# Attention and a gated two-layer product: wide differences from GpSimd to VectorE, wider fillers, one score step moved

## The chip, the cores and the metric

The kernel runs on one core of one Trainium2 chip. Its engines are TensorE (PE in the profile; PEld is its loading of weights), VectorE (DVE), ScalarE (ACT), GpSimd (POOL) and SyncE (SP), whose queue issues nearly all DMA transfers. The metric is the device time of one execution in microseconds (us); lower is better. The time before is 831.21 us, the median of three runs (831.0 to 831.5).

## The reference

Block-local softmax attention on 8 batches, 8 heads, 576 positions in chunks of 64, then a gated product on its result, all in float32:

```
scores = scale * matmul(q_c, k_c^T)                # per chunk of 64
attn   = exp(scores - max) ; attn = attn / (sum + 1e-9)
x      = matmul(attn, v_c)                         # 4608 tokens x 512
h      = x @ w_in                                  # 512 x 2048
g      = h * clip(h + 3, 0, 6) / 6
out    = g @ w_out                                 # 2048 x 512
```

## The kernel before

Precision comes from splitting: each operand is kept as a high part (a cast to fp32r on ACT) and a low part (operand minus high part, on DVE), and `passes` (L295 to L299) runs three matmuls per pair, high by high (L297), high by low (L298), low by high (L299). One such 128x512 matmul starts 0.227 us after the one before when PE runs freely; six of them make one part of a product, 1.36 us.

The 4608 tokens are nine blocks of 512. Each block has two attention units, named by block and half ("61" is the second half of block 6). A unit is a chain of steps: scores on PE (L222), maximum, difference (L229, L233) on DVE, exponential on ACT, sum with reciprocal, share (L240 to L245) on DVE, a transpose on PE (L255, "turn"), a copy on ACT (L259), the product with the values on PE (L273), and a copy to keep it (L280 or L283 on ACT, for the first three blocks also a residue, L286 on DVE).

Blocks 0 to 2 then go through the two matrix products tile by tile: sixteen tiles of weights (L166 loads them, `convert` makes high and low parts on ACT and DVE, the low part at L193), a first product a/b, a gate, a second product c. Blocks 3 to 8 are taken two at a time, in three stages s = 0, 1, 2, with seven products in place of eight for a 2x2 scheme of quarters. That costs additions and differences: of the operands x (`x_steps`, L432: four differences of 1024 columns in each stage), of the gated values (L687 and L689, 512 columns, on POOL; L711 on DVE and L714 on POOL, 1024 columns, four each in each stage), and of the results. Each operand of the second product is split by `add_units`: high on ACT (L704), low on DVE (L708). So a stage is a first product (56 parts, f), a change to the second product, and the second product (56 parts, s). While a stage changes over, one attention unit for the next stage is under way: unit 61 in stage 0, unit 81 in stage 1, none in stage 2.

In stage 0 the differences L432 run on DVE, in stages 1 and 2 on POOL; L714 runs on POOL in all three.

The order on each engine is made at build time. Every step is entered in a table with its engine, an assumed cost, what it waits for, and a due time; `Schedule.order` goes through them as a list scheduler does, and the instructions are then issued in that order. An assumed cost thus changes no instruction, but it can change the order. The engines run their own lists in order; they wait for each other only through data and buffers. SP's list is fixed the same way; the load of the next unit's q and k waits until the scores of the unit before have been computed, because there is one buffer.

Ahead of the first weight tile PE also runs fillers ("products on nothing", `warm_up`, L154): 11 at the very start, on zeros, 512 columns wide, and then a number in each of PE's planned pauses, `int(FILL * pause)`, with 256 columns of the identity.

Of the kernel before, what the change touches and what calls it, by code (L numbers as in the profile page):

```python
# [9 lines left out]
F32 = mybir.dt.float32  # L10
F32R = mybir.dt.float32r
BF16 = mybir.dt.bfloat16
# [3 lines left out]
ALU = mybir.AluOpType  # L16
AX = mybir.AxisListType

P = 128
# [4 lines left out]
NT = NB * CH  # L24
# [9 lines left out]
SLOTS = 7 * NFP  # L34
HALF = [slice(0, CH), slice(CH, P)]
WARM = 11
FILL = 6.5
LAG = 2
EDGE = 32
HASTE = 5.0  # L40
# [72 lines left out]
def tile_kernel(ctx: ExitStack, tc: tile.TileContext, qk_in, v_in, weights, out):  # L113
    nc = tc.nc
    PE, ACT, DVE, POOL = nc.tensor, nc.scalar, nc.vector, nc.gpsimd
# [8 lines left out]
    ps_h = pool("ps_h", 2, space=bass.MemoryType.PSUM)  # L124
# [10 lines left out]
    op = None  # L135

    nought = rp.tile([P, NT], F32, name="r")
    POOL.memset(nought, 0.0)
    ident = const.tile([P, P], F32, name="ident")
# [4 lines left out]
    ACT.activation(out=warm, in_=half, func=AF.Exp)  # L144


    some = ident.bitcast(BF16)

    def warm_up(n, a=some, b=some):
        if not n:  # L150
            return
        idle = ps_h.tile([P, NT], F32, name="h")[:, :b.shape[-1]]
        for _ in range(n):
            PE.matmul(idle, lhsT=a[:, :P], rhs=b, start=True, stop=True)  # L154

    nought = nought.bitcast(BF16)
    warm_up(WARM, nought, nought[:, P:P + 512])

# [262 lines left out]
    def operand():  # L423
        return xop_pool.tile([P, 2, 2, NT], F32R, name="xop")

    WHERE = {1: (0, 0), 5: (0, 1), 6: (0, 1), 7: (0, 0), 2: (1, 0), 3: (1, 1), 4: (0, 1)}

    def x_steps(s, eng):
        n = NSTD + 2 * s
        b = lambda i, j: xraw[n + j][:, i]  # L430
        name = lambda i: f"x{s}.{i}"
        minus = lambda to, x, y: lambda: eng.tensor_tensor(out=b(*to), in0=b(*x), in1=b(*y), op=ALU.subtract)  # L432
        sub = ("DVE", 1.3) if eng is DVE else ("POOL", 2.9)
        ops[s] = {}
        last = name("s0")
        steps = [(last, *sub, [], minus((0, 1), (0, 1), (0, 0)), [0, 1])]

        def high(i):
            ops[s][i] = operand()
            ACT.copy(out=ops[s][i][:, :, 0], in_=b(*WHERE[i]))  # L440

        def lower(i):
            DVE.tensor_tensor(out=ops[s][i][:, :, 1], in0=b(*WHERE[i]), in1=ops[s][i][:, :, 0].bitcast(F32), op=ALU.subtract)

        for i in ORDER_A:
            reads = {2: [3], 3: [2]}.get(i, [])
            steps.append((name(f"{i}h"), "ACT", 1.05, [last], lambda i=i: high(i), reads))
            steps.append((name(f"{i}l"), "DVE", 1.35, [name(f"{i}h")], lambda i=i: lower(i), []))
            for k, at, to, x, y, reads in (("s1", 5, (0, 1), (1, 1), (0, 1), [2]), ("s2", 6, (0, 0), (0, 1), (0, 0), []),
                                           ("s3", 6, (0, 1), (1, 0), (0, 1), [3])):  # L450
                if i == at:
                    steps.append((name(k), *sub, [name(f"{i}l"), name("1l"), last], minus(to, x, y), reads))
                    last = name(k)
        return steps
# [4 lines left out]
    work = Schedule()  # L459
# [7 lines left out]
    def attention(u, due, scores=(), less=(), keep=()):  # L467
        n, dp = int(u[0]), int(u[1])
        a = heads[u]
        steps = [("scores", "PE", 1.30, a.scores, ["qk" + u, *scores]), ("max", "DVE", 1.23, a.largest, ()),  # L470
                 ("less", "DVE", 1.23, lambda: a.lessen(spare.get("e" + u, lambda: None)()), less), ("exp", "ACT", 1.06, a.exp, ()),
                 ("sum", "DVE", 1.68, a.total, ()), ("share", "DVE", 1.22, a.share, ()), ("turn", "PE", 1.07, a.turn, ()),
                 ("turned", "ACT", 1.02, a.turned, ()), ("product", "PE", 1.50, a.product, ["v" + u]), ("keep", "ACT", 1.03, a.keep, keep)]
        if n < NSTD:
            steps.append(("rest", "DVE", 1.23, a.rest, ()))
        before = None
        for name, engine, cost, f, more in steps:
            before = work.add(name + u, engine, cost, [before, *more], f, due=due)
        return before
# [7 lines left out]
    due_of = {"10": 13 * STEP, "11": 15 * STEP, "20": 24 * STEP, "21": 28 * STEP}  # L487
    for s in range(NSUP):
        n = NSTD + 2 * s
# [3 lines left out]
    prior = dict(zip(chain[1:], chain))  # L493
    for k, name in enumerate(LOADS):
        part, u = name.rstrip("0123456789"), name.lstrip("qkvw")
# [8 lines left out]
    made = {"00": attention("00", 1e9), "01": attention("01", 1e9)}  # L504
# [4 lines left out]
    for u in chain[1:]:  # L509
        n = int(u[0])  # L510
        s = (n - NSTD) // 2
        free = () if n == 1 else [f"b{NFT - 1}"] if n == 2 else [f"b{2 * NFT - 1}"] if s == 0 else [f"x{s - 1}.{i}l" for i in ORDER_A]
        attention(u, due_of[u], [made[prior[u]]] if n > 1 or u[1] == "1" else (), ["product" + prior[u]], free)

    for ft in range(NFT):
        free = lambda step: f"{step}{ft - 2}" if ft > 1 else None
        up, shift, down, join, high, lower = convert(ft)
# [7 lines left out]
    def tile_steps(n, ft):  # L525
        t = {}

        def first():
            t["h"] = ps_h.tile([P, NT], F32, name="h")
            mm1_half(n, ft, t["h"], 0)  # L530

        def second():
            mm1_half(n, ft, t["h"], 1)
            t["of"], t["steps"] = gate_steps(t["h"])

        return (first, second, *[lambda k=k: t["steps"][k]() for k in range(4)], lambda *ets: [mm2(ft, t["of"]["g"], et) for et in ets],
                lambda et: store(n, et, acc[et])())

    for j, (n, ft) in enumerate(mm):
        first, second, relu, gate, high, lower, sums, send = tile_steps(n, ft)  # L540
# [11 lines left out]
        for et in range(NET):  # L552
            name = f"c{j}" if et == NET - 1 else f"c{j}.{et}"
# [31 lines left out]
    for u in range(2 * NFP):  # L585
        whole, combine, high, lower, send, send_own = sum_steps(u % 2, u // 2)
# [105 lines left out]
    def add_units(s):  # L692
        both = lambda name, pp: [f"{name}{s}.{2 * pp + k}" for k in range(2)]
        made_by = {1: "gate2.", 5: "t1.", 6: "t2.", 2: "gate4.", 3: "gate7."}
        for i in ORDER_B:
            for pp in range(NFP // 2):
                high, low = f"uh{s}.{i}.{pp}", f"ul{s}.{i}.{pp}"
                r, c = WHERE[i]
                src = lambda i=i, pp=pp, r=r, c=c: t2_of[s][pp] if i == 6 else g_of[s][pp][:, r, c]
                after = both(made_by[i], pp) if i in made_by else [f"m{s}.{i}.{pp}"]  # L700

                def top(i=i, pp=pp, src=src):
                    g_ops[s, i, pp] = operand()
                    ACT.copy(out=g_ops[s, i, pp][:, :, 0], in_=src())  # L704

                work.add(high, "ACT", 1.05, [*after, *work.take("xop", 8, high, [f"s{s}.{NFP * ORDER_B.index(i) + 2 * pp + 1}"
                         if not (s == NSUP - 1 and i == 3) else f"s{s}.{SLOTS - 4 + pp}"])], top)
                work.add(low, "DVE", 1.35, [high], lambda i=i, pp=pp, src=src: DVE.tensor_tensor(  # L708
                    out=g_ops[s, i, pp][:, :, 1], in0=src(), in1=g_ops[s, i, pp][:, :, 0].bitcast(F32), op=ALU.subtract))
                if i == 5:  # L710
                    work.add(f"m{s}.7.{pp}", "DVE", 1.35, [f"ul{s}.1.{pp}", *both("t2.", pp)], lambda pp=pp: DVE.tensor_tensor(  # L711
                        out=g_of[s][pp][:, 0, 0], in0=t2_of[s][pp], in1=g_of[s][pp][:, 0, 0], op=ALU.subtract))
                elif i == 6:
                    work.add(f"m{s}.4.{pp}", "POOL", 2.9, [f"ul{s}.5.{pp}", *both("t2.", pp), *both("gate4.", pp)], lambda pp=pp: POOL.tensor_tensor(  # L714
                        out=g_of[s][pp][:, 0, 1], in0=g_of[s][pp][:, 1, 0], in1=t2_of[s][pp], op=ALU.subtract))

    def second_product(s):
# [63 lines left out]

    for s in range(NSUP):
        first = [u for u in chain if (int(u[0]) - NSTD) // 2 == s and int(u[0]) >= NSTD]
        for name, engine, cost, after, f, reads in x_steps(s, DVE if s == 0 else POOL):
            if name.endswith("h"):
                i = int(name[-2])
                after = [*after, "free", *work.take("xop", 8, name, [f"f{i}.{s}.{NFP - 1}"])]
            work.add(name, engine, cost, [*after, *[made[first[k]] for k in reads]], f)
        first_product(s)
        add_units(s)  # L790
        second_product(s)
# [4 lines left out]
    idle = {products[k][0]: products[k + 1][1] - products[k][2] for k in range(until)}  # L796
    for name, _ in listed:
        if name == "c0.0":
            banks.close()
            ps_o = pool("ps_o", 4, space=bass.MemoryType.PSUM)  # L800
        work.steps[name][3]()
        warm_up(int(FILL * idle.get(name, 0.0)))
    order.close()
# [26 lines left out]
```

## Time and profile before

| what | value |
|---|---|
| median of three runs | 831.21 us |
| the profiled execution's own time | 831.62 us |
| its span in the profile | 829.8 us |
| mean granted TensorE clock | 0.985 |
| PE, DVE, ACT, POOL busy | 800.2, 625.4, 365.7, 132.5 us |
| POOL at L714, 1024 columns | 12 of 3376 ns, 40.2 us |
| POOL at L432, 1024 columns | 8 of 2661 ns, 21.3 us |
| POOL at L687 and L689, 512 columns | 24 of 1413 ns and 24 of 1505 ns |
| fillers at L154 after the first 11 | 62 of 256 columns |

The span is what the profiler saw of the program; the time of the same execution is 1.8 us longer. In a timeline a row gives start, duration, engine, line, operation, output <- inputs, shape and count; in brackets stands how long the engine had been idle and what released it. In a windows row the columns are the stretch, its length, the busy time of PE, PEld, DVE, ACT and POOL (with instructions), the granted clock of PE, the busy share of the DMA engines and GB/s.

### The profile page before, as it was taken

To read this page: it belongs to the slowest core of one execution; us is meant where nothing else is said; L and a number is where in the kernel's file an instruction comes from. 1 tells how busy PE (TensorE), PEld (TensorE's weight loads), DVE (VectorE), ACT (ScalarE), POOL (GpSimd) and SP (SyncE) were. 2 spreads that over 40 slices of the span, in tenths; PEclk is the share of its full clock that TensorE was granted. 3 is DMA by queue.
4 is the path that set the end of the run, shared out by engine and by line. 5 is a ranking of instruction groups with operands and counts; after the bars stand their busy time and mean duration, and the time that the engine had idled before them with its cause. 6 is when DMAs were issued, how large, how long until landed. Compare 5 with 4: busy or idle time off the path is not lost.

```text
span 829.8 us, 13676 instructions
## 1 busy us (share of the span) xinstructions
PE 800.2 (96%) x5689; PEld 655.2 (79%) x5689; DVE 625.4 (75%) x751; ACT 365.7 (44%) x453; POOL 132.5 (16%) x76
## 2 busy tenths in 40 slices
PE   7899999999999999999996999999959999999998
PEld 5688888888888888888875888888848888888886
DVE  6798988798875556776997666869977677679961
ACT  4888744434433434344724443335433433336330
POOL 0000000000000001222350032221900123227100
PEclk9999999999999999999997999999979999999999
DMA  9970399964655113465762766656626575555563
GB/s 366 410 315 1 89 358 354 322 215 146 218 202 212 43 63 142 178 229 203 254 227 96 260 226 244 228 200 231 236 83 213 196 231 201 200 180 205 198 225 131
DMA packets 50158, 172.86 MB, mean 208 GB/s; under 512 B 4656, under 2 KB 17200, under 8 KB 39344
## 3 DMA queue, kind: packets, MB, share of 16 engines
q1 hardware_dynamic: 49952, 171.85, 58.3%
q8 instruction: 45, 0.74, 0.4%
q14 instruction: 17, 0.14, 0.1%
q10 hardware_dynamic: 144, 0.13, 0.0%
HBM read 133.17 MB, written 38.80 MB: 207 GB/s over the span
## 4 chain that ended last, share of the span: by engine, by line
PE 84%; DVE 11%; DMA 2%; issue 1%; ACT 1%; SPq 0%; DVEq 0%; ACTq 0%
PE acc L297 17%; PE acc L298 17%; PE acc L299 17%; PE h L297 9%; PE h L299 9%; PE h L298 9%; DVE xop L708 6%; PE two L273 2%; PE two L255 2%; DMA w<-w_in_out 2%; PE two L222 2%; DVE g L621 1%; DVE g L711 1%; DVE z L240 1%; DVE e L245 1%
## 5 line engine op out<-in xcount | busy, mean ns | idle before, releaser
L297 PE MATMUL acc<-xop,ws 128*128 128x512 f32 x528 | 207.5, 393 | 0.0
L299 PE MATMUL acc<-xop,ws 128*128 128x512 f32 x528 | 205.6, 389 | 0.0
L298 PE MATMUL acc<-xop,ws 128*128 128x512 f32 x528 | 205.6, 389 | 0.0
L708 DVE TENSOR_TENSOR xop<-g,xop 128x1024 fp32r<-128x1024 f32 x72 | 104.6, 1471 | 27.1 <-ACT xop L704 27.0
L297 PEld LDWEIGHTS acc<-xop,ws 128*128 128x128 f32 x528 | 99.1, 188 | 21.1 <-DVE u L611 0.2
L299 PEld LDWEIGHTS acc<-xop,ws 128*128 128x128 f32 x528 | 99.1, 188 | 20.8
L687 POOL TENSOR_TENSOR g<-g 128x512 f32<-128x512 f32 x24 | 33.9, 1413 | 510.8 <-PE acc L299 327.0
L298 PEld LDWEIGHTS acc<-xop,ws 128*128 128x128 f32 x528 | 99.1, 188 | 19.9
L704 ACT CAST xop<-g 128x1024 fp32r<-128x1024 f32 x72 | 74.0, 1052 | 89.5 <-PE acc L299 39.4
L297 PE MATMUL h<-x,w 128*128 128x512 f32 x192 | 77.6, 404 | 0.4 <-ACT w L190 0.4
L299 PE MATMUL h<-x,w 128*128 128x512 f32 x192 | 75.7, 394 | 0.5 <-DVE w L193 0.5
L298 PE MATMUL h<-x,w 128*128 128x512 f32 x192 | 75.5, 393 | 0.0
L297 PE MATMUL acc<-g,w 128*128 128x512 f32 x192 | 75.0, 391 | 0.0
L299 PE MATMUL acc<-g,w 128*128 128x512 f32 x192 | 74.7, 389 | 0.0
L298 PE MATMUL acc<-g,w 128*128 128x512 f32 x192 | 74.7, 389 | 0.0
L618 ACT ACTIVATE r<-acc,half 128x512 f32<-128x512 f32 x72 | 49.2, 687 | 37.9 <-DVE acc L611 37.5
L312 ACT ACTIVATE r<-h,half 128x512 f32<-128x512 f32 x48 | 33.0, 689 | 74.0 <-PE h L299 74.0
L618 ACT ACTIVATE r<-h,half 128x512 f32<-128x512 f32 x24 | 16.5, 689 | 102.6 <-DVE h L611 102.6
L297 PE MATMUL h<-xop,ws 128*128 128x512 f32 x144 | 57.7, 400 | 0.0
L298 PE MATMUL h<-xop,ws 128*128 128x512 f32 x144 | 56.8, 395 | 0.0
L299 PE MATMUL h<-xop,ws 128*128 128x512 f32 x144 | 56.8, 394 | 0.0
L621 DVE SCALAR_TENSOR_TENSOR g<-r,acc 128x512 f32<-128x512 f32 x72 | 48.9, 680 | 6.2 <-ACT r L618 6.1
(88 smaller groups left out, 1248.6 us busy)
## 6 DMA issues: line engine op xcount, KB each, us to landing
ws<-b SPq DMA_DIRECT2D x42, 1024.0 KB, 4.9
ws<-a SPq DMA_DIRECT2D x24, 1024.0 KB, 4.8
ws<-a SPq DMA_DIRECT2D x24, 768.0 KB, 4.2
qk<-qk_in SPq DMA_DIRECT2D x17, 1024.0 KB, 5.8
w<-w_in_out SPq DMA_DIRECT2D x16, 1024.0 KB, 16.2
v<-v_in SPq DMA_DIRECT2D x17, 512.0 KB, 4.8
a<-hl SPq DMA_DIRECT2D x32, 256.0 KB, 3.6
b<-hl SPq DMA_DIRECT2D x32, 256.0 KB, 3.8
```

What stands on the lines that cost most here:

```text
L222: PE.matmul(self.s[o, a, c, :], lhsT=self.qk[rows, 0, c, o], rhs=self.qk[rows, 1, c, o], start=True, stop=True)
L255: PE.transpose(out=self.tp[:, a, i], in_=self.e[:, a, 2 * i:2 * i + 2].rearrange("p c t -> p (c t)"), identity=ident)
L273: PE.matmul(po[o, s, a, i, :], lhsT=self.v[rows, a, i, o], rhs=self.aT[rows, a, i, o], start=True, stop=True)
L297: PE.matmul(ps, lhsT=a_h, rhs=b_h, start=first, stop=False, skip_group_check=more)
L298: PE.matmul(ps, lhsT=a_h, rhs=b_l, start=False, stop=False, skip_group_check=more)
L299: PE.matmul(ps, lhsT=a_l, rhs=b_h, start=False, stop=last, skip_group_check=more)
L312: ACT.activation(out=t["r"], in_=h, func=AF.Relu, bias=half, scale=1.0 / 6.0)
L618: ACT.activation(out=t["r"], in_=ps(), func=AF.Relu, bias=half, scale=1.0 / 6.0)
L621: work.add("gate" + name, "DVE", 0.69, ["relu" + name], lambda: DVE.scalar_tensor_tensor(out=out(), in0=t["r"], scalar=1.0, in1=ps(), op0= ...
L687: work.add(id_("t1."), "POOL", 1.45, [id_("gate3."), id_("gate2.")], lambda f=gq: POOL.tensor_tensor(out=f(0, 1), in0=f(0, 1), in1=f(0, 0) ...
L704: ACT.copy(out=g_ops[s, i, pp][:, :, 0], in_=src())
L708: work.add(low, "DVE", 1.35, [high], lambda i=i, pp=pp, src=src: DVE.tensor_tensor(out=g_ops[s, i, pp][:, :, 1], in0=src(), in1=g_ops[s, i ...
```

## The change

Four things are edited. First, the differences at L432 (stages 1 and 2) and at L714 (all stages) go to DVE. Second, assumed costs of 1024-column DVE steps become 1.22 in place of 1.3 and 1.35, which with the moved steps changes the planned order in some places. Third, every filler multiplies zeros, with 512 columns, and `FILL` goes from 6.5 to 3.2, so that there are about half as many. Fourth, the first scores of block 1 (unit 10) wait for b0, the second half of the first tile's first product, where they waited for nothing but their data.

```diff
-FILL = 6.5
+FILL = 3.2
...
-    some = ident.bitcast(BF16)
-
-    def warm_up(n, a=some, b=some):
-        if not n:
-            return
-        idle = ps_h.tile([P, NT], F32, name="h")[:, :b.shape[-1]]
-        for _ in range(n):
-            PE.matmul(idle, lhsT=a[:, :P], rhs=b, start=True, stop=True)
-
     nought = nought.bitcast(BF16)
-    warm_up(WARM, nought, nought[:, P:P + 512])
+
+    def warm_up(n):
+        if n:
+            idle = ps_h.tile([P, NT], F32, name="h")
+            for _ in range(n):
+                PE.matmul(idle, lhsT=nought[:, :P], rhs=nought[:, P:P + NT], start=True, stop=True)
+
+    warm_up(WARM)
...
-    def x_steps(s, eng):
+    def x_steps(s):
...
-        minus = lambda to, x, y: lambda: eng.tensor_tensor(out=b(*to), in0=b(*x), in1=b(*y), op=ALU.subtract)
-        sub = ("DVE", 1.3) if eng is DVE else ("POOL", 2.9)
+        minus = lambda to, x, y: lambda: DVE.tensor_tensor(out=b(*to), in0=b(*x), in1=b(*y), op=ALU.subtract)
+        sub = ("DVE", 1.22)
...
-            steps.append((name(f"{i}l"), "DVE", 1.35, [name(f"{i}h")], lambda i=i: lower(i), []))
+            steps.append((name(f"{i}l"), "DVE", 1.22, [name(f"{i}h")], lambda i=i: lower(i), []))
...
-        attention(u, due_of[u], [made[prior[u]]] if n > 1 or u[1] == "1" else (), ["product" + prior[u]], free)
+        attention(u, due_of[u], [made[prior[u]]] if u != "10" else ["b0"], ["product" + prior[u]], free)
...
-                work.add(low, "DVE", 1.35, [high], lambda i=i, pp=pp, src=src: DVE.tensor_tensor(
+                work.add(low, "DVE", 1.22, [high], lambda i=i, pp=pp, src=src: DVE.tensor_tensor(
...
-                    work.add(f"m{s}.7.{pp}", "DVE", 1.35, [f"ul{s}.1.{pp}", *both("t2.", pp)], lambda pp=pp: DVE.tensor_tensor(
+                    work.add(f"m{s}.7.{pp}", "DVE", 1.22, [f"ul{s}.1.{pp}", *both("t2.", pp)], lambda pp=pp: DVE.tensor_tensor(
...
-                    work.add(f"m{s}.4.{pp}", "POOL", 2.9, [f"ul{s}.5.{pp}", *both("t2.", pp), *both("gate4.", pp)], lambda pp=pp: POOL.tensor_tensor(
+                    work.add(f"m{s}.4.{pp}", "DVE", 1.22, [f"ul{s}.5.{pp}", *both("t2.", pp), *both("gate4.", pp)], lambda pp=pp: DVE.tensor_tensor(
...
-        for name, engine, cost, after, f, reads in x_steps(s, DVE if s == 0 else POOL):
+        for name, engine, cost, after, f, reads in x_steps(s):
```

The changed kernel's line numbers are lower by 2 from L160 on.

What this does to the order is shown at two places. The first is DVE's list where stage 0 changes over, from the low part of the last t operand to the sum of unit 61's softmax. The names are tiles: xop an operand being split, g and t gated values, two the scores, m and e, z the softmax. Before:

```order
L708 TENSOR_TENSOR xop<-t_3224,xop 128x2x512
L708 TENSOR_TENSOR xop<-g_3217,xop 128x2x512
L708 TENSOR_TENSOR xop<-g_3218,xop 128x2x512
L711 TENSOR_TENSOR g_3219<-t_3223,g_3219 128x1024
L711 TENSOR_TENSOR g_3220<-t_3224,g_3220 128x1024
L708 TENSOR_TENSOR xop<-g_3219,xop 128x2x512
L708 TENSOR_TENSOR xop<-g_3220,xop 128x2x512
L229 TENSOR_REDUCE m<-two 128x16
L233 TENSOR_TENSOR e<-two,m 128x1024
L708 TENSOR_TENSOR xop<-g_3217,xop 128x2x512
L240 TENSOR_REDUCE z<-e 128x16
```

The same place on DVE in the changed kernel (tile numbers differ, L712 is L714 of before, now on this engine):

```order
L706 TENSOR_TENSOR xop<-t_3189,xop 128x2x512
L709 TENSOR_TENSOR g_3183<-t_3187,g_3183 128x1024
L706 TENSOR_TENSOR xop<-g_3182,xop 128x2x512
L709 TENSOR_TENSOR g_3184<-t_3188,g_3184 128x1024
L706 TENSOR_TENSOR xop<-g_3183,xop 128x2x512
L709 TENSOR_TENSOR g_3185<-t_3189,g_3185 128x1024
L706 TENSOR_TENSOR xop<-g_3184,xop 128x2x512
L712 TENSOR_TENSOR g_3182<-g_3182,t_3186 128x1024
L706 TENSOR_TENSOR xop<-g_3185,xop 128x2x512
L227 TENSOR_REDUCE m<-two 128x16
L231 TENSOR_TENSOR e<-two,m 128x1024
L706 TENSOR_TENSOR xop<-g_3182,xop 128x2x512
```

The first L709 stood one row higher up before; one L712 has come in ahead of the softmax of unit 61, and the other three, with the moved x differences, stand behind its last step. In stage 1 the same place has one more L709 (the last of its four) ahead of unit 81's last step than before, and all four L712 behind it. On PE the transpose of unit 61 and that of unit 60 each stand one part of the second product earlier, and the values product of unit 60 two parts earlier; on ACT the copy of unit 60's transpose stands ahead of the last two relus of the first product. SP's list is the same.

The second place is PE's list at the start: the values product of unit 00 (L273), the transpose of unit 01 (L255), and what follows. Before, the scores of unit 10 (L222; this list counts 32 instructions where the profile counts 64 matmuls) come next, then five fillers, of which the first is shown:

```order
L154 MATMUL h<-ident 128x256
L273 MATMUL two<-e,v 64x64 x32
L255 MATMUL two<-ident,g 128x128 x8
L222 MATMUL two<-qk 64x64 x32
L154 LDWEIGHTS ident
L154 MATMUL h<-ident 128x256
```

In the changed kernel PE goes from the transpose straight to the fillers, six of them, now 512 columns of zeros:

```order
L153 MATMUL h<-r 128x512
L271 MATMUL two<-e,v 64x64 x32
L253 MATMUL two<-ident,g 128x128 x8
L153 LDWEIGHTS r
L153 MATMUL h<-r 128x512
```

The scores of unit 10 stand behind the first two weight tiles' first product (w_373 is the second tile, w_456 the third):

```order
L295 MATMUL h<-x,w_373 128x512
L296 MATMUL h<-x,w_373 128x512
L297 MATMUL h<-x,w_373 128x512
L220 MATMUL two<-qk 64x64 x32
L295 MATMUL h<-x,w_456 128x512
L296 MATMUL h<-x,w_456 128x512
L297 MATMUL h<-x,w_456 128x512
```

So 64 score matmuls and, over the whole start, 28 of 62 fillers have left the stretch ahead of the first weight tile.

## The prediction

> **What bounds the kernel now.** I read the page's busy shares first, then the list of waits for TensorE alone, then its timeline wherever it waits.
>
> ```profile
> PE 800.2 (96%) x5689; PEld 655.2 (79%) x5689; DVE 625.4 (75%) x751; ACT 365.7 (44%) x453; POOL 132.5 (16%) x76
> PE two L255 <- DVE e L245: 20.4, 3, 9.4
> PE two L273 <- issue: 1.7, 1, 1.7
> ```
>
> TensorE (PE) is busy 96% of the span, so a change pays only where PE waits or runs slowly. Three waits for the softmax's last VectorE step (L245) in front of transposes (L255) make up 20.4 us; the smallest (1.75) is at the start. The timeline places the two large ones, and a window shows the clock there:
>
> ```profile
> 442.95 1.94 PE L255 MATMUL two<-ident,e 128*128 128x128 f32 x8 [9.26 <-DVE e L245]
> 448.12 0.50 PE L297 MATMUL acc<-xop,ws 128*128 128x512 f32 x1
> 612.57 1.94 PE L255 MATMUL two<-ident,e 128*128 128x128 f32 x8 [9.37 <-DVE e L245]
> 619.57 0.50 PE L297 MATMUL h<-xop,ws 128*128 128x512 f32 x1
> 437.00:438.00 1.00, 0.00 (x0) 0.00 (x0) 0.97 (x2) 0.00 (x0) 0.00 (x0) 0.50 0.00 0
> ```
>
> PE stands still from 433.69 to 442.95 (stall A) and from 603.20 to 612.57 (stall B), the two places where a first product gives way to a second while an attention unit is in flight. During A the granted clock falls to 0.50, and the work behind runs at half speed until 448. Why was VectorE (DVE) late? Here are GpSimd (POOL) and DVE ahead of A and of B:
>
> ```profile
> 408.29 2.16 POOL L689 TENSOR_TENSOR t<-g 128x512 f32<-128x512 f32 x1
> 410.41 13.40 POOL L714 TENSOR_TENSOR g<-g,t 128x1024 f32<-128x1024 f32 x4
> 423.76 3.37 POOL L432 TENSOR_TENSOR x<-x 128x1024 f32<-128x1024 f32 x1
> 579.95 2.53 POOL L432 TENSOR_TENSOR x<-x 128x1024 f32<-128x1024 f32 x1 [9.06 <-ACT x L280]
> 586.92 13.38 POOL L714 TENSOR_TENSOR g<-g,t 128x1024 f32<-128x1024 f32 x4
> 407.36 7.52 DVE L708 TENSOR_TENSOR xop<-g,xop 128x1024 fp32r<-128x1024 f32 x3
> 414.80 10.09 DVE L708 TENSOR_TENSOR xop<-t,xop 128x1024 fp32r<-128x1024 f32 x3
> 424.81 3.40 DVE L711 TENSOR_TENSOR g<-t,g 128x1024 f32<-128x1024 f32 x1
> 428.13 1.21 DVE L708 TENSOR_TENSOR xop<-t,xop 128x1024 fp32r<-128x1024 f32 x1
> 429.27 2.34 DVE L708 TENSOR_TENSOR xop<-g,xop 128x1024 fp32r<-128x1024 f32 x2
> 441.58 1.23 DVE L245 TENSOR_TENSOR e<-e,z 128x1024 f32<-128x1024 f32 x1
> 591.30 10.09 DVE L708 TENSOR_TENSOR xop<-t,xop 128x1024 fp32r<-128x1024 f32 x3
> 611.20 1.22 DVE L245 TENSOR_TENSOR e<-e,z 128x1024 f32<-128x1024 f32 x1
> L432 POOL TENSOR_TENSOR x<-x x8: 2387/2408/3383, 423.8 to 666.0; 128x1024 f32<-128x1024 f32 x8
> ```
>
> While POOL works through 1024 columns, a DVE difference lasts 10.09 / 3 = 3.36 us and a POOL one 13.40 / 4 = 3.35: they take turns. The same DVE line on the same operand takes 1.21 at 428.13, when POOL has stopped, and starts 1.14 apart from the next (429.27 - 428.13). A wide POOL difference at its fastest takes 2.39 (the least of the last row), and with 1 us of DVE ahead of it that is 3.4. So every wide POOL difference costs a DVE neighbour 3.35 - 1.14 = **2.2 us**. The Trainium skill, SBUF — State Buffer, section "Who interferes with whom", says the same as a lock: a VectorE instruction with two SBUF inputs and a GpSimd instruction that reads SBUF exclude one another for a whole instruction, and the trace agrees (3.36 beside 3.35).
>
> **Wide differences to DVE, stall A.** Five wide POOL differences go from the stretch (four L714, one L432). DVE loses five slow slots: the last of the three at 407.36, the three at 414.80, the one at 424.81. That is 5 x 2.2 = 11.0 us. The narrow POOL pair that ends with the 2.16 stays, and so does its cost. In the new order one of the moved differences stands ahead of the softmax's last step: +1.14. The transpose can then start at 442.95 - 11.0 + 1.14 = 433.1. PE arrives one part of the product earlier than before, since the transpose has moved up one place: six matmuls x 0.227 = 1.36, so 433.69 - 1.36 = 432.3. One thing makes it later. The transpose of the unit before also moves up one part, ahead of its data:
>
> ```profile
> 404.17 1.03 PE L255 MATMUL two<-ident,e 128*128 128x128 f32 x8
> 402.11 1.21 DVE L245 TENSOR_TENSOR e<-e,z 128x1024 f32<-128x1024 f32 x1
> 541.69 0.87 PE two L255 x8
> ```
>
> It would be reached at 404.17 - 1.36 = 402.8, and its data end at 403.3: a new wait of 0.5 us on PE, with all of the second product queued behind it; on ACT the copy L259 now stands ahead of two relus (L618), which end some 0.6 us later, still before PE's banks are asked for. So PE arrives at 432.8 and waits 0.3. From 433.1: transpose 0.87 (chain row), two parts 2.72, the values product 1.09 (448.12 less its start at 447.02), end at 437.8 against 448.12. **A gives 10.3 us**, of which about 2 is the clock that no longer drops.
>
> **Stall B.** Four slow slots go (the L714 four): 8.8 us. The wide difference at 579.95 goes too, but the narrow pair behind it moves up into its place; I take 0.5 between nothing and 1.0. One more difference stands ahead of the last step: +1.14. So 612.57 - 8.8 - 0.5 + 1.14 = 604.4, PE arrives at 603.2 and waits 1.2. Then 0.87 + 2.72 + 1.09 end at 609.1 against 619.57: **B gives 10.5 us**. With no wait left A would give 11.1 and B 11.7; with 2 us more on DVE in each, 8.3 and 8.5.
>
> **What the moved work costs elsewhere.** DVE takes 20 differences, 12 at L714 and 8 at L432, some 20 x 1.14 = 23 us, and gets about as much back. The third change of product has no attention unit; PE never waits there:
>
> ```profile
> 760.00:770.00 10.00, 10.00 (x46) 8.29 (x45) 10.00 (x4) 3.19 (x4) 10.00 (x4) 1.00 0.57 199
> 499.68 0.69 DVE L611 TENSOR_TENSOR u<-h,p 128x512 f32<-128x512 f32 x1 [2.40 <-PE h L299]
> ```
>
> That window also shows PE at full rate with DVE and POOL both full, so this stage gives nothing. The differences of the next stage's operands (L432) now queue on DVE between the residues (L443). The product that needs the third operand ends only at 499.68, and the operand was ready by 486.3; I cost them at nothing, with 10 us of cover. At the end nothing moves.
>
> **The start.** PE, then the clock, ACT and SP's queue:
>
> ```profile
> 20.27 1.09 PE L255 MATMUL two<-ident,g 128*128 128x128 f32 x8
> 21.29 1.16 PE L222 MATMUL two<-qk 64*64 64x64 f32 x64
> 22.39 0.72 PE L154 MATMUL h<-ident 128*128 128x256 bf16 x5
> 23.04 0.33 PE L273 MATMUL two<-g 64*64 64x64 f32 x5
> 25.10 1.15 PE L273 MATMUL two<-g 64*64 64x64 f32 x59 [1.73 <-issue]
> 33.88 0.50 PE L297 MATMUL h<-x,w 128*128 128x512 f32 x1 [0.35 <-ACT w L190]
> 35.14 0.50 PE L299 MATMUL h<-x,w 128*128 128x512 f32 x1 [0.53 <-DVE w L193]
> 28.00:29.00 1.00, 1.00 (x4) 0.73 (x3) 1.00 (x2) 1.00 (x2) 0.00 (x0) 0.50 1.06 414
> 21.94 1.05 ACT L259 COPY g<-two 128x1024 f32<-128x1024 f32 x1
> 32.21 0.69 ACT L312 ACTIVATE r<-h,half 128x512 f32<-128x512 f32 x1 [1.74 <-PE h L299]
> 24.13 0.70 SPq L210 DMA_DIRECT2D qk<-qk_in  x1
> 24.87 17.96 SPq L166 DMA_DIRECT2D w<-w_in_out  x7
> ```
>
> Five of 64 products of unit 01 run at 23.04, then PE waits 1.73 us for nothing that the profile shows ("issue"): I take it for the instruction stream running late after a dense burst. Ahead of that point the change takes out 64 score matmuls with their weight loads and 28 of the 62 fillers. The fillers that remain there are 6 of 512 columns, 6 x 0.23 to 0.26 = 1.4 to 1.6 us, so 21.36 to 22.9: they still fit before the copy at 21.94 has ended (22.99). Without the gap the values product ends at 24.2, not 26.2: 2.0 us. The half clock from 26.8 to 30.2 follows the gap; if it goes as well, 1.6 us more. What is late next is the residue L286 of unit 01, ready near 26.5, when PE wants it at 26.9; then the third weight tile, whose conversion on ACT waits behind the relu at 32.21, itself released by PE, and so moves with PE. The wait at 35.14 becomes one near 31.5: **3.6 us**. The moved scores (1.1 us) stand just ahead of that tile's first matmul and fill the waits for it (0.35 ahead of 33.88 and 0.53 ahead of 35.14), so at most 0.3 us of them is left over; were the tile ready sooner, they would cost their 1.1. The load of the next q and k (24.13) waits for these scores and goes to about 31, and seven weight loads stand behind it in SP's queue. The DMA engines still have work then: 13.5 loads of 1 MiB (14.2 MB) were issued before 24.1, which at the 0.414 MB per us of the window above last to 34 at least. So the loads cost nothing. Bounds: 0, if the gap stays or moves, to 3.8.
>
> The Trainium skill, TensorE: Matmul & The Clock Gate, section "What's actually happening", says that the clock halves after an idle window of about 3.4 us and that the window runs freely. For stall A the trace agrees (9.26 us, then 0.50). A gap of 1.73 would be too short by that figure, though the trace shows 0.50 behind it; by the rule the half clock could stay when the gap goes, and the start would give 2.0 instead of 3.6.
>
> **Sum.** 10.3 + 10.5 + 3.6 = 24.4. The profiled execution took 831.62 us (span 829.8), 0.41 over the median 831.21. 831.21 - 24.4 = **806.8 us**.
>
> **Rivals.**
>
> 1. The start gives nothing: the gap moves to another burst. For it: one gap in the whole trace is a matter of phase. Against it: the burst becomes shorter. 831.2 - 20.8 = 810.4. Chance 0.2. With the gap gone and the half clock left, 808.4; that is inside the forecast.
> 2. The stalls go only in part: what remains on POOL (narrow pairs at 2.16) takes more turns, or DVE's added work gathers before the softmax, 2 to 5 us in each. 831.2 - 3.6 - (20.8 - 4 to 10) = 811 to 817. Against it: the new position of DVE leaves one extra instruction ahead of each last step, no more. Chance 0.12.
> 3. Slower: the 3.36 us is DVE's own price for these operands and not POOL's. Then nothing is freed and each transpose waits for one more difference, 1.14 to 3.4, with 0.5 at the unit before: 831.2 + 2.8 to 7.3 = 834 to 838.5. It decides as soon as a softmax's last step ends later than 442.8 or 612.4. The row at 428.13 (same line, 1.21) speaks against it. Chance 0.03.
> 4. The change does nothing, because DVE's gain and load cancel ahead of the two steps (within 0.2%): 0.02.
>
> The forecast, 804.5 to 809.5, has 0.63. **Range** 804.2 to 812: the low end is A and B without any wait and the start at 3.8, the high end the start at nothing and a microsecond more at each stall. 0.2% (1.7 us) is about what a measurement of this kernel can tell from no change. Faster 0.95, same 0.02, slower 0.03.
>
> **What would show it.** Right: L708 on xop<-t near 1.2 us everywhere, no POOL instruction of 1024 columns, waits of PE for L245 summing to under 5 us, granted clock 1.00 around both places, no "issue" wait in front of L273 at the start, and the first weight tile's matmuls (L297, right behind the values product that ends at 26.2) 2 to 4 us earlier. Wrong: wide DVE differences that stay at 3 us, PE waits of several us at the two transposes, or a new PE wait in the first product.

## The result and the profile after

The changed kernel takes **806.83 us** (median of 4 runs, 806.76 to 806.95) against 831.11 us for the kernel before (830.88 to 831.5): a ratio of 0.9708, 95% interval 0.9691 to 0.9724. The forecast was 806.8. The profiled execution took 806.82 us, with a span of 805.0.

The page's busy shares and the list of TensorE's waits, which answer to the first lines of the prediction (L253 is L255 of before, L243 is L245, L271 is L273):

```profile
PE 794.2 (99%) x5658; PEld 647.9 (80%) x5661; DVE 612.6 (76%) x771; ACT 367.0 (46%) x453; POOL 71.3 (9%) x56
PE two L253 <- DVE e L243: 3.0, 3, 1.7
```

PE is busy 99% of a shorter span, and its waits for the softmax fell from 20.4 us to 3.0; the largest of the three, 1.7, is the one at the start. DVE has 20 instructions more and is nonetheless busy 13 us less in sum (625.4 before): it took 20 differences over and lost more than that in slow slots. Around the two changes of product, PE first, then DVE in the stretch ahead of A:

```profile
399.54 1.06 PE L253 MATMUL two<-ident,e 128*128 128x128 f32 x8 [0.51 <-DVE e L243]
429.10 1.06 PE L253 MATMUL two<-ident,e 128*128 128x128 f32 x8
432.87 1.16 PE L271 MATMUL two<-e,v 64*64 64x64 f32 x64
433.96 0.50 PE L295 MATMUL acc<-xop,ws 128*128 128x512 f32 x1
589.88 1.06 PE L253 MATMUL two<-ident,e 128*128 128x128 f32 x8 [0.81 <-DVE e L243]
593.62 1.16 PE L271 MATMUL two<-e,v 64*64 64x64 f32 x64
594.71 0.50 PE L295 MATMUL h<-xop,ws 128*128 128x512 f32 x1
403.48 5.31 DVE L706 TENSOR_TENSOR xop<-g,xop 128x1024 fp32r<-128x1024 f32 x3
408.72 4.62 DVE L706 TENSOR_TENSOR xop<-t,xop 128x1024 fp32r<-128x1024 f32 x4
420.07 1.21 DVE L712 TENSOR_TENSOR g<-g,t 128x1024 f32<-128x1024 f32 x1
427.73 1.22 DVE L243 TENSOR_TENSOR e<-e,z 128x1024 f32<-128x1024 f32 x1
```

Four differences on xop<-t now last 4.62 us together, where three had lasted 10.09. The three on xop<-g ahead of them still take 5.31, since the narrow POOL pair (L685, L687) runs beside them. The moved difference (L712) takes 1.21 on DVE; on POOL it took 3.35. The softmax of unit 61 ends at 428.95, and PE's transpose follows with no wait in the list. The groups, by line and shape, say the same for the whole span:

```profile
L712 DVE TENSOR_TENSOR g<-g,t 128x1024 f32<-128x1024 f32 x12 | 14.4, 1216 | 0.0
L706 DVE TENSOR_TENSOR xop<-t,xop 128x1024 fp32r<-128x1024 f32 x12 | 14.0, 1212 | 0.0
L430 DVE TENSOR_TENSOR x<-x 128x1024 f32<-128x1024 f32 x12 | 14.6, 1220 | 2.3 <-ACT x L278 2.2
```

The start, as PE's timeline has it:

```profile
21.42 1.24 PE L153 MATMUL h<-r 128*128 128x512 bf16 x5
23.01 1.16 PE L271 MATMUL two<-g 64*64 64x64 f32 x64 [0.35 <-ACT g L257]
24.10 0.50 PE L295 MATMUL h<-x,w 128*128 128x512 f32 x1
29.78 1.16 PE L220 MATMUL two<-qk 64*64 64x64 f32 x64
31.47 0.50 PE L297 MATMUL h<-x,w 128*128 128x512 f32 x1
28.00:29.00 1.00, 1.00 (x6) 0.82 (x5) 1.00 (x2) 0.82 (x2) 0.00 (x0) 1.00 1.06 422
```

The values product runs in one piece, the first tile starts at 24.10 where it started at 26.17, and the clock stays at 1.00.

### The profile page after: what moved, and what is told of

The parts are those of the page before. It is cut to its first block, busy times and chain, and to the rows that moved or that the text cites. A ratio compares the mean times of both kernels' runs of the same rounds, so it can differ in the third digit from the quotient of the medians.

```text
span 805.0 us, 13605 instructions
## 1 busy us (share of the span) xinstructions
PE 794.2 (99%) x5658; PEld 647.9 (80%) x5661; DVE 612.6 (76%) x771; ACT 367.0 (46%) x453; POOL 71.3 (9%) x56
## 4 chain that ended last, share of the span: by engine, by line
PE 93%; DVE 3%; DMA 2%; ACT 1%; issue 1%; SPq 0%; DVEq 0%; ACTq 0%
PE acc L295 20%; PE acc L296 19%; PE acc L297 19%; PE h L295 10%; PE h L297 9%; PE h L296 9%; PE two L271 2%; PE two L220 2%; PE two L253 2%; DMA w<-w_in_out 2%; DVE xop L706 1%; DVE g L709 0%; DVE e L243 0%; DVE z L238 0%; ACT r L616 0%
## 5 line engine op out<-in xcount | busy, mean ns | idle before, releaser
L706 DVE TENSOR_TENSOR xop<-g,xop 128x1024 fp32r<-128x1024 f32 x72 | 95.4, 1335 | 21.1 <-ACT xop L702 21.0
L685 POOL TENSOR_TENSOR g<-g 128x512 f32<-128x512 f32 x24 | 34.0, 1416 | 658.2 <-DVE g L619 335.1
L295 PE MATMUL h<-xop,ws 128*128 128x512 f32 x144 | 56.4, 392 | 0.0
L297 PE MATMUL h<-xop,ws 128*128 128x512 f32 x144 | 56.1, 389 | 0.0
L296 PE MATMUL h<-xop,ws 128*128 128x512 f32 x144 | 56.1, 389 | 0.0
```

The lines of the kernel that those rows point to most:

```text
L295: PE.matmul(ps, lhsT=a_h, rhs=b_h, start=first, stop=False, skip_group_check=more)
L296: PE.matmul(ps, lhsT=a_h, rhs=b_l, start=False, stop=False, skip_group_check=more)
L297: PE.matmul(ps, lhsT=a_l, rhs=b_h, start=False, stop=last, skip_group_check=more)
L685: work.add(id_("t1."), "POOL", 1.45, [id_("gate3."), id_("gate2.")], lambda f=gq: POOL.tensor_tensor(out=f(0, 1), in0=f(0, 1), in1=f(0, 0) ...
L706: work.add(low, "DVE", 1.22, [high], lambda i=i, pp=pp, src=src: DVE.tensor_tensor(out=g_ops[s, i, pp][:, :, 1], in0=src(), in1=g_ops[s, i ...
```

## The experiments

The theory is that DVE and POOL take turns when both run differences, that this held the softmax up at A and B, and that the start is a term of its own. Each run is compared with runs of the kernel before on the same chip, taken in turn with it.

**The differences alone.** The changed kernel with the start of before:

```diff
-FILL = 3.2
+FILL = 6.5
...
-        attention(u, due_of[u], [made[prior[u]]] if u != "10" else ["b0"], ["product" + prior[u]], free)
+        attention(u, due_of[u], [made[prior[u]]] if n > 1 or u[1] == "1" else (), ["product" + prior[u]], free)
```

(and `warm_up` as before).

> The changed kernel with the start of before (256-column fillers of the identity, FILL 6.5, block 1's first scores ahead of the first tile); differences and assumed costs as changed. If the terms add up, this keeps the two terms at the changes of product and loses the start's 3.9 us: 810.8 us (0.975). If the start's gain came from the moved differences, 806.8; if the stalls shrank because everything ran earlier, above 815.

Measured: 808.99 us, 0.9743 (0.9726 to 0.9759). The terms at the changes of product stand without the start. But the start lost only some 2.2 us, not 3.9. The reason is in this run's own start, PE and then the window of the clock:

```profile
25.20 1.15 PE L273 MATMUL two<-g 64*64 64x64 f32 x59 [1.56 <-issue]
33.63 0.50 PE L299 MATMUL h<-x,w 128*128 128x512 f32 x1 [0.53 <-DVE w L193]
28.00:29.00 1.00, 1.00 (x6) 0.84 (x5) 1.00 (x2) 1.00 (x2) 0.00 (x0) 1.00 1.06 422
```

The gap is there (1.56 us), and the clock is not halved behind it. In the profile of before the same wait for the third tile stood at 35.14; here it stands at 33.63 although the gap ends 0.1 us later. So a gap alone does not bring the half-clock spell of 1.6 us.

**The start alone.** The kernel before with the changed `warm_up`, `FILL` and wait of unit 10's scores, and nothing else.

> The kernel before with only the changed start (512-column fillers of zeros, FILL 3.2, scores behind b0). Adding up: 831.1 - 3.9 = 827.2, with the waits of 9.3 and 9.4 us at the two transposes as before. If the two parts help each other, above 829.

Measured: 828.87 us (827.23 to 829.54) beside 831.46 (829.18 to 833.18): 0.9967 (0.9956 to 0.9978), or 2.6 us where 3.9 was expected. Gap and spell are both absent from its profile. The times of the kernel before spread over 4 us here, which is what a spell that comes and goes would do to them. The mean granted clock of those 13 runs points the same way: it is 0.985 in eight (831.2 to 833.2 us) and 0.987 in five (829.2 to 831.5), and 3.4 us at half clock are 0.002 of the span; with the changed start all ten runs have 0.987 or 0.989. In which stretch of a single run the clock was low is not on record, so the spell itself is argued here and not shown.

**Only the x differences moved.** The changed kernel with L712 back on POOL:

```diff
-                    work.add(f"m{s}.4.{pp}", "DVE", 1.22, [f"ul{s}.5.{pp}", *both("t2.", pp), *both("gate4.", pp)], lambda pp=pp: DVE.tensor_tensor(
+                    work.add(f"m{s}.4.{pp}", "POOL", 2.9, [f"ul{s}.5.{pp}", *both("t2.", pp), *both("gate4.", pp)], lambda pp=pp: POOL.tensor_tensor(
```

> The changed kernel with the gated differences (four per stage) back on GpSimd; the x differences stay on VectorE. Turn taking: four slow slots of 2.2 us come back at each change of product, the transposes wait about 9 us again and the clock drops: 826 to 829. If the planned order did the work (it is the changed one here but for the place of one difference), 807 to 809.

Measured: 827.33 us, 0.9962 (0.9947 to 0.9977). The stalls are back; PE's timeline has 8.78 us ahead of unit 61's transpose and 9.60 ahead of unit 81's, and the transposes run at half clock (1.94 us for eight):

```profile
437.92 1.94 PE L253 MATMUL two<-ident,e 128*128 128x128 f32 x8 [8.78 <-DVE e L243]
609.02 1.94 PE L253 MATMUL two<-ident,e 128*128 128x128 f32 x8 [9.60 <-DVE e L243]
```

8.78 is four slots of 2.2, and 9.60 is the 0.81 of the changed kernel and four more. The planned order is nearly that of the changed kernel, so the order is not what brings the gain.

**Only the gated differences moved.** The changed kernel with L430 back on POOL in stages 1 and 2 (`x_steps(s, DVE if s == 0 else POOL)`, as before).

> The changed kernel with the x differences (four in each of stages 1 and 2) back on GpSimd; the gated differences stay on VectorE. Turn taking: one wide GpSimd difference falls ahead of each transpose, at most 2.2 us each and no drop of the clock: 808.5 to 811. If the x differences were what held VectorE, above 815.

Measured: 810.74 us (809.55 to 811.52), 0.9758 (0.9741 to 0.9776). The waits are 2.17 and 1.70 us, against none and 0.81 in the changed kernel, and the clock holds:

```profile
431.50 1.06 PE L253 MATMUL two<-ident,e 128*128 128x128 f32 x8 [2.17 <-DVE e L243]
593.15 1.06 PE L253 MATMUL two<-ident,e 128*128 128x128 f32 x8 [1.70 <-DVE e L243]
```

So at A one wide POOL difference ahead of the transpose costs one slot of 2.2 us. At B the wait is 0.9 longer than in the changed kernel; the prediction put this term at 0.5, between nothing and 1.0.

**The start taken apart.** First the fillers alone (the changed `warm_up` and `FILL` in the kernel before), then the scores alone:

```diff
-        attention(u, due_of[u], [made[prior[u]]] if n > 1 or u[1] == "1" else (), ["product" + prior[u]], free)
+        attention(u, due_of[u], [made[prior[u]]] if u != "10" else ["b0"], ["product" + prior[u]], free)
```

> The kernel before with only the fillers changed (512 columns of zeros, FILL 3.2); block 1's first scores stay ahead of the first tile. If the 1.73 us gap in front of the values product comes from many instructions in a short time, 28 fillers fewer may not be enough, since the 64 scores stay: gap stays, 831; if the fillers alone cause it: 827 to 829.

> The kernel before with only block 1's first scores moved behind b0; fillers as before. If the burst of scores and fillers causes the gap, it goes: 827 to 828. If the gap comes at a fixed number of instructions, it appears some 190 instructions later, in the first tile or later, and the time is 829 to 831.

Measured: 829.74 us, 0.9983 (0.9974 to 0.9992), and 829.24 us, 0.9985 (0.9976 to 0.9993), beside 831.07. Neither removes the gap; each moves it. PE at the values product, of the fillers alone (first two rows) and of the scores alone:

```profile
23.06 0.80 PE L271 MATMUL two<-g 64*64 64x64 f32 x37
25.20 0.68 PE L271 MATMUL two<-g 64*64 64x64 f32 x27 [1.34 <-issue]
```

```profile
23.15 1.15 PE L273 MATMUL two<-g 64*64 64x64 f32 x61 [0.24 <-ACT g L259]
25.34 0.33 PE L273 MATMUL two<-g 64*64 64x64 f32 x3 [1.04 <-issue]
```

The gap came after 5 of the 64 products before; now it comes after 37 and after 61. It is not set off by a burst. Counted in the traces, 350 weight loads stand ahead of the gap in every profile that has it: before, differences alone, order alone, fillers alone, scores alone. With the scores gone (64 loads) and eight fillers more at that place, 56 loads fewer stand ahead of this product, and 5 + 56 = 61. In the run with the fillers alone 30 planned fillers are left of 62, 32 fewer, and 5 + 32 = 37. The expectation of a fixed number of instructions held, though with the scores alone the place is 56 pairs of load and matmul further on and not some 190 instructions. So the gap sits at a fixed number of instructions, and PE always goes on at nearly the same time: 25.10 before, then 25.20 (differences alone), 25.20 and 25.34. That is how a wait for the next piece of the instruction stream would look. The traces hold a transfer that fits: one 16 KB packet on the DMA queue of kind "instruction" (q8), which starts at 22.6 to 22.8 us and takes 1.0 to 1.1 in all five. PE goes on 1.2 to 1.5 us after it has landed; that PE waits for this packet is likely and not shown. Only when both edits are made does that place lie behind the values product: the changed kernel gets to its 350th load at 29.9, long after the same packet (22.6) has landed, and has nothing to wait for.

**Work that nobody waits for, reading.** The changed kernel plus eight POOL differences of 448 columns per stage into a spare tile:

```diff
+                    work.add(f"d{s}.4.{pp}", "POOL", 2.9, [f"ul{s}.5.{pp}", *both("t2.", pp), *both("gate4.", pp)], lambda pp=pp: [POOL.tensor_tensor(
+                        out=spare_out, in0=g_of[s][pp][:, 1, 0, k, :448], in1=t2_of[s][pp][:, k, :448], op=ALU.subtract) for k in range(2)])
```

> The changed kernel plus work that nothing waits for: where the gated differences stood on GpSimd, eight differences of 448 columns per stage that read the same tiles and write a spare one. Turn taking: each costs VectorE about 1 us ahead of the transposes, so the waits return to 8 us or so and the clock drops: 822 to 828. If GpSimd held the kernel up through what waited for its results, 806.8 to 807.5.

Measured: 825.71 us, 0.9943 (0.9928 to 0.9958): 18.9 us lost to results that nothing uses. POOL and DVE ahead of A, and PE's two waits:

```profile
406.60 16.81 POOL L715 TENSOR_TENSOR dummy<-g,t 128x448 f32<-128x448 f32 x8
409.75 8.46 DVE L707 TENSOR_TENSOR xop<-t,xop 128x1024 fp32r<-128x1024 f32 x4
436.80 1.94 PE L253 MATMUL two<-ident,e 128*128 128x128 f32 x8 [7.62 <-DVE e L243]
608.03 1.94 PE L253 MATMUL two<-ident,e 128*128 128x128 f32 x8 [8.46 <-DVE e L243]
```

16.81 / 8 = 2.10 and 8.46 / 4 = 2.12: again one instruction each, in turn. A DVE difference loses 1 us to a POOL difference of 448 columns, and 2.2 to one of 1024. Eight of them are 7.7 us, which is the wait at A (7.62) and the growth of the wait at B (8.46 - 0.81).

**The same, writing only.** Twenty memsets per stage in the place of the eight differences:

```diff
+                    work.add(f"d{s}.4.{pp}", "POOL", 2.9, [f"ul{s}.5.{pp}", *both("t2.", pp), *both("gate4.", pp)], lambda: [POOL.memset(spare_out, 0.0) for _ in range(5)])
```

> The changed kernel plus GpSimd work that only writes: where the gated differences stood, twenty memsets of 448 columns per stage, about 9 us of GpSimd time, as much as the dummy differences that read. If VectorE and GpSimd exclude each other only where GpSimd reads, VectorE's differences stay at 1.2 us and the time at 806.8 to 807.5. If any GpSimd instruction takes its turn, 815 to 828.

Measured: 806.85 us, 0.9705 (0.9686 to 0.9723), the changed kernel's time. POOL is busy through the same stretch, and DVE does not notice:

```profile
406.49 10.57 POOL L715 MEMSET dummy<- 128x448 f32 x20
408.69 4.62 DVE L707 TENSOR_TENSOR xop<-t,xop 128x1024 fp32r<-128x1024 f32 x4
```

What takes turns is work that reads, not POOL's being busy; a POOL instruction that reads only one operand was not tried. The Trainium skill, SBUF — State Buffer, section "Who interferes with whom", says that a VectorE instruction with two SBUF inputs contends with a GpSimd instruction that reads SBUF and not with one that only writes; both runs agree.

**The order alone.** The kernel before with only the assumed costs changed (1.35 and 1.3 to 1.22):

```diff
-            steps.append((name(f"{i}l"), "DVE", 1.35, [name(f"{i}h")], lambda i=i: lower(i), []))
+            steps.append((name(f"{i}l"), "DVE", 1.22, [name(f"{i}h")], lambda i=i: lower(i), []))
```

(and the three other places).

> The kernel before with only the assumed costs of VectorE's 1024-column steps changed (1.22), all differences where they were. The order then puts one more difference ahead of unit 61's and unit 81's last softmax step, and unit 61's transpose one part earlier, with GpSimd still in VectorE's way: about 1 us more wait at each, and up to 1.4 us of PE work that no longer stands ahead of the first wait: 833 to 836. If the new order helps by itself, below 830.

Measured: 834.18 us, 1.0039 (1.0025 to 1.0053), a little slower. The waits at the two transposes grow to 9.96 and 10.50 us. With POOL still in the way, the new order puts one instruction more ahead of the softmax and one part less ahead of the wait.

**What is left.** Two runs on the changed kernel: the narrow differences (L685, L687) on DVE too, and another assumed cost for the last softmax step of units 60 and 81.

```diff
-                        work.add(id_("t1."), "POOL", 1.45, [id_("gate3."), id_("gate2.")], lambda f=gq: POOL.tensor_tensor(
+                        work.add(id_("t1."), "DVE", 0.69, [id_("gate3."), id_("gate2.")], lambda f=gq: DVE.tensor_tensor(
...
-                        work.add(id_("t2."), "POOL", 1.45, [id_("t1."), id_("gate7.")], lambda f=gq, p=p: POOL.tensor_tensor(
+                        work.add(id_("t2."), "DVE", 0.69, [id_("t1."), id_("gate7.")], lambda f=gq, p=p: DVE.tensor_tensor(
```

> The changed kernel with the narrow differences (512 columns, 16 per stage) on VectorE too, so that GpSimd has no work in the stages. VectorE takes 48 more of about 0.6 us, 29 us, in stretches where it is 60 to 70% busy, and loses the last slow slots (about 1 us each ahead of the transposes). The two waits that are left, 0.5 and 0.8 us, are the most it can give: 806 to 807.5. If VectorE becomes the bound at the changes of product, 808 to 812.

```diff
+SLACK = {"60": 1.0, "81": 1.0}
...
-                 ("sum", "DVE", 1.68, a.total, ()), ("share", "DVE", 1.22, a.share, ()), ("turn", "PE", 1.07, a.turn, ()),
+                 ("sum", "DVE", 1.68, a.total, ()), ("share", "DVE", 1.22 + SLACK.get(u, 0.0), a.share, ()), ("turn", "PE", 1.07, a.turn, ()),
```

> The changed kernel with 1.0 us more assumed for the last softmax step of units 60 and 81, which should let the planner place the scores of both units one part of the product earlier, and so their last step ahead of need. The two waits left (0.5 and 0.8 us) go at best: 805.5 to 806.5. If the maximum and difference then wait for nothing sooner because VectorE is full, 806.8.

Measured: 804.94 us (804.64 to 805.11), 0.9681 (0.9665 to 0.9696), and 805.99 us (805.96 to 806.01), 0.9694 (0.9678 to 0.9709), both taken in turn with the kernel with memsets, which took 806.85. All on DVE is the fastest version of this study and beats both kernels; it beat its expectation (806 to 807.5) too. Its page and PE's list of waits:

```profile
PE 793.8 (99%) x5658; PEld 648.3 (81%) x5661; DVE 633.6 (79%) x819; ACT 366.4 (46%) x453; POOL 1.2 (0%) x8
PE two L253 <- DVE e L243: 1.9, 1, 1.9
```

DVE takes 48 more differences for 21 us more of busy time, and only the wait at the start is left. It gave 1.9 us where I had put the two remaining waits, 1.3, as the most. The other 0.6 lies at the same places: from the changed kernel's profile to this one, the scores behind unit 60's transpose start 0.64 us earlier (420.92 and 420.28), those behind unit 61's 0.92 (580.88 and 579.96), and those behind unit 81's 1.90 (613.98 and 612.08). So each transpose had held PE up by more than its listed wait, that of unit 61 by 0.3 with none listed.

The other assumed cost did what it was meant to. PE's timeline has no wait at either transpose and a new one of 0.54 us behind a DVE step (at 392.81, released by L610): 1.3 less 0.5 is 0.8, and the time fell by 0.9.

## Why the prediction came out

**Stall A** was put at 10.3 us. Between the two profiles, the matmul behind unit 61's values product moved from 448.12 to 432.87 + 1.09 = 433.96, 14.16 us. What came before A is read from the maximum of unit 60 on DVE, first in the profile of before, then in that of after:

```profile
394.45 1.21 DVE L229 TENSOR_REDUCE m<-two 128x16 f32<-128x1024 f32 x1
```

```profile
390.52 1.22 DVE L227 TENSOR_REDUCE m<-two 128x16 f32<-128x1024 f32 x1
```

It moved by 3.93. A gave 14.16 - 3.93 = **10.2**. The steps hold one by one: slots of 2.2 (the runs with L712 or L430 back on POOL show them at 4 x 2.2 and 2.2), one more difference at 1.14, the new wait of 0.5 at unit 60 (0.51). The remaining wait of 0.3 at the transpose is in no list, though the run with all on DVE gains 0.3 at this place.

**Stall B** was put at 10.5. The matmul behind unit 81's product went from 619.57 to 594.71, 24.86 us, less 14.16: **10.7**. The wait that was left is 0.81 where 1.2 was expected. The term that was too small is the 0.5 for the wide difference at 579.95: with the 0.9 that the run with only the gated differences moved shows, 612.57 - 8.8 - 0.9 + 1.14 = 604.0, 0.8 after PE.

**The start** was put at 3.6 and gave 3.7 at the third tile's matmul and 3.9 by the time of unit 60. Size and end points are right: this matmul was put near 31.5 and stands at 31.47 (35.14 before). The cause was partly wrong. In "the instruction stream running late after a dense burst" the burst fell: the gap keeps its place in the instructions (350 weight loads) and its end in time (25.0 to 25.3), whatever runs ahead. The instruction stream is still the likely cause. The gap went because two edits together pushed that place behind the values product; one alone shifts it. That the gap went was partly luck: the reason given was a shorter burst, and what counted was that both edits together took enough instructions away. "The half clock follows the gap" holds only in part: two profiles with a gap show 0.50 at 28 us (before, order alone), three show 1.00 (differences alone, fillers alone, scores alone), and none of the eight without a gap shows it. The 3.9 is therefore about 2.1 for the gap (24.10 against 26.17), some 1.6 for a spell that the profile of before happened to have, and 0.2 to 0.3 later on. The 2.2 us between the differences alone (808.99) and the changed kernel (806.83, measured at another time) and the 2.6 of the start alone lie between the two.

Why the spell came and went can be followed further in the traces. In the profile of before the granted clock changes at 26.68, 30.10, 436.28, 446.52, 606.95 and 617.19 us. All are whole multiples of 3.413 us apart, so in this trace the clock changes only at the ends of steps of that length, and the other profiles have the same steps from another starting point. Counted back or on from these changes, the gap lies whole in one step in the profiles of before (1.73 us between 23.27 and 26.68) and of the order alone (1.64), and the step behind it is the one at 0.50. It also lies in one step where only the fillers or only the scores changed, but is shorter (1.34 and 1.04); in the differences alone a step ends at 24.3 inside it, so at most 0.9 us of it fall in one. In these three the clock holds. Idle time is not all that counts: with only the gated differences moved, PE stood for 1.74 us of the step from 429.76 to 433.17, and the clock stayed at 1.00. The rule on the clock that the prediction quoted from the Trainium skill (TensorE: Matmul & The Clock Gate, section "What's actually happening"), that the window runs freely, agrees with these steps. A whole idle window of 3.4 us does not: half a step was enough in two profiles, and what else must come together is not shown.

**The other costs** were put at nothing and were: from 24 us on, the changed kernel's PE has no listed wait but those at units 60 and 81. So the third change of product has none, the next stage's operands come in time, and the loads behind the moved scores hold nothing up.

**The rivals.** That 3.36 us was DVE's own price is refuted by the same line at 1.21 on the same operands. That the stalls would go only in part is refuted by the waits (none and 0.81). That the gap would move and the start give nothing is half right: with either edit alone the gap does move, and the gain shrinks to between 1 and 2 us (1.3 for the fillers, 1.8 for the scores, by the medians). The ends of the range come to 804.6 and 812.4 by the terms that were named for them, where 804.2 and 812 were written.

## What to carry to other kernels

When differences on VectorE last the sum of two engines' times, look at what GpSimd reads meanwhile; the price of an "idle" GpSimd's work stands in VectorE's rows, and matters where VectorE holds TensorE up. Moving work onto the busier engine can leave it less busy. An unexplained wait early in a program should be watched at two positions, with the instructions ahead of it counted in each, before it is put down to what runs there.

## What was not expected of the hardware

PE's gap at the start ended at 25.0 to 25.3 us in five programs (25.02 in the one with the order alone), always behind 350 weight loads: after 5 of the 64 products in three and after 37 and 61 in two. It kept its number of instructions, not its place in the work. The clock fell to 0.50 for one step of 3.4 us behind a gap of 1.73 and of 1.64 us, and not behind two shorter ones (1.34 and 1.04) and one that a step's end divided. And POOL, busy for 10.57 us with memsets beside DVE's two-operand differences, cost them nothing (4.62 us for four with and without).
